# Retention plus gated MLP on one core: a hand-set engine order, two heads' scores on the row halves of TensorE, and the decay folded into q and v

## The chip, the cores and the metric

The kernel runs on one core of one Trainium2 chip. The metric is the device time of one execution in microseconds (us). Fast executions of one kernel agree within 1.5% here. The kernel before took 274.74 us in the median of four runs of one session (273.62 to 276.08). "Ratio" below means the mean time of the fast runs of one kernel over the mean of the fast runs of the kernel before, taken in the same rounds on the same chip. It is therefore not quite the ratio of the medians that are quoted beside it.

PE is TensorE (matmul on an array of 128 x 128), PEld its weight loads, PSUM is where the kernel puts the results of matmuls, DVE is VectorE, ACT is ScalarE, POOL is GpSimd, and SP is the engine that issues loads.

## The reference, cut to what matters

```python
# q, k, v: (8 batches, 8 heads, 576 positions, 64)
scores = (1/sqrt(64)) * q @ k.T
gamma  = 1 - 2.0 ** (-5 - arange(8))                  # one decay per head
ret    = scores * where(rel >= 0, gamma ** rel, 0)    # rel = query position - key position
x      = (ret @ v), heads side by side                # (8, 576, 512)

h      = gelu_tanh(x @ w_in)                          # 512 -> 1024
u, vv  = halves of h
v_n    = (vv - mean) / sqrt(var + 1e-6) * g_ln
v_s    = einsum('ts,bsd->btd', w_sg, v_n) + b_sg      # mixes the 576 positions of a batch
out    = x + (u * v_s) @ w_out
```

The decay is separable: gamma^(t-s) is gamma^t times gamma^(-s). So it can be multiplied into q, v or the result, and only the triangular mask remains for the scores.

## The kernel before: the parts that the change and the argument touch

Two batches make a pair of 9 tiles of 128 positions, and 4 pairs make 36 tiles. The fifth tile of a pair (the middle tile) straddles the two batches. Each tile passes through the following blocks, and the document uses their names throughout:

- `tp`: transposes of q and k; `sc`: scores; `ret`: masked scores, made by DVE.
- `ot`: attention output in PSUM, with one part from the carried state (`zbd`) and one from `ret` and v; `zp`: the update of the state.
- `hv` and `hu`: the two halves of the first MLP product; `vg`, `vn` (in a middle tile `vmid`): gelu and normalization of `hv`.
- `wp`: the product with w_sg, possible only once the 5 tiles of a batch are normalized; `gT`: its product with `uT`; `op`: the output.
- `wT`: the transposed w_sg, built once at the start in ten pieces, each with TensorE transposes (`wtp`) and a copy by DVE.

```python
def attn_T(i):                       # one tile: 8 transposes, then three copies out of PSUM
    ...
    nc.vector.tensor_copy(qT[:], tp[:, 0, :, :])
    nc.scalar.activation(kbd[:64, :, 0, :], tp[:64, 1, :, :], Act.Copy)   # zero-padded keys
    nc.vector.tensor_copy(kbd[64:, :, 1, :], tp[64:, 1, :, :])

def attn_S(i):                       # 8 heads in two PSUM tiles of 4, each masked by DVE
    for j in range(2):
        sc = psS.tile([128, 4, 128], F32, name="sc", tag="sc")
        for r in range(4):
            kk, hh = 2 * j + r // 2, r % 2
            nc.tensor.matmul(sc[:, r, :], s["kbd"][:, kk, hh, :], s["qT"][:, kk, :], ...)
        nc.vector.tensor_tensor(ret[:, 4*j:4*j+4, :], sc[:], msk..., op=Alu.mult)

def attn_O(i):                       # state part and two zero-padded v matmuls per head pair
    for kk in range(KK):
        nc.tensor.matmul(ot[:, kk, :n], st["zbd"][:, kk, :], s["qT"][:, kk, :n], ...)
        for hh in range(2):
            nc.tensor.matmul(ot[:, kk, :], s["vp"][:, 2*kk+hh, :], s["ret"][:, 2*kk+hh, :], ...)
    nc.vector.tensor_tensor(xT..., ot[:], ttab..., op=Alu.mult)           # decay of the queries

def build_rows():                    # rows 1/g_ln and b_sg for the w_sg product, all on DVE
    nonzero(row4[:, 0, :F2], row_t[:, :F2])                 # three passes over 4x512
    nc.vector.reciprocal(row4[:, 0, :F2], row4[:, 0, :F2])
    ...                                                     # casts and selections, 4x512, 4x576
    for t in vmid: nc.sync.dma_start(...row4b...)           # DMA them into vmid and wT

# ...
for i in range(N + 3):               # program order; the framework's scheduler reorders it
    flush(i)
    if i == SB: build_rows()
    ...loads, prep...
    attn_S(i); mlp_V(i - 1); two build_wT; attn_T(i + 1); mlp_U(i - 1); attn_O(i); attn_Z(i)
    run(2)                           # two queued units of mlp_W (two PSUM tiles) or mlp_O
```

## Time and profile before

| | before |
|---|---|
| time, median (4 runs) | 274.74 us |
| span of the profiled run | 272.1 us |
| PE busy | 227.3 us, 84% |
| DVE / ACT / POOL busy | 189.2 / 130.1 / 128.1 us |
| start of `hv` of the 8th tile | 77.4 us |
| start of `hv` of the 36th tile | 251.6 us, so 6.22 us per tile over 28 tiles |
| from there to the end | 20.5 us |

The start times of `hv` serve as a clock for the program: there is one `hv` per tile, and in steady state the distance between two of them is the time of one iteration. They cut the run into a head (up to the 8th tile), a steady part of 28 tiles, and a tail. In the kernel before the first eight start at 18.0, 23.3, 32.7, 45.3, 52.7, 60.5, 72.7 and 77.4 us.

The page of the kernel before begins with its span, the busy times, and 40 slices of the span. A digit is the busy share of a slice in tenths, and PEclk is the granted TensorE clock in tenths.

```profile
span 272.1 us, 6371 instructions
PE 227.3 (84%) x2498; PEld 171.3 (63%) x2498; DVE 189.2 (70%) x405; ACT 130.1 (48%) x230; POOL 128.1 (47%) x244
...
PE   0477747869899899987999899879998999889893
...
PEclk9999595999999999999999999999999999999998
```

After the first quarter PE is at 8 or 9 in most slices. The average of 84% hides a head in which PE is the waiting engine.

The timeline of PE in the kernel before shows one steady iteration. Columns: start in us, duration, engine, line, operation, `out<-in`, tile of the array, shape, type, count. Ends are modelled and overlap the next start, so the cost of a block is read from start to start.

```profile
101.59 0.61 PE L251 MATMUL sc<-qT,kbd_168 128*128 128x128 bf16 x8
102.04 1.03 PE L307 MATMUL hv<-w_in,xT 128*128 128x512 bf16 x4
...
104.24 0.22 PE L267 MATMUL ot<-qT,zbd_171 128*128 128x128 bf16 x1
...
104.91 0.39 PE L289 MATMUL zp<-vpad_165,qkb 128*128 128x128 bf16 x4
```

`sc` costs 102.04 - 101.59 = 0.45 us and the whole of `ot` 104.91 - 104.24 = 0.67 us. Eight full-array matmuls of 128 columns take 0.45 us, so one takes 0.056 us. These are the two blocks that the change puts on half arrays.

The table of waits of the kernel before (total us, times, longest us) has this line for the start of a `wp` block:

```profile
PE wp L349 <- DVE gT L354: 5.9, 6, 1.1
```

About 1 us is lost where such a block begins. In the head the chain of waits (start, duration, what) runs over DVE, where the row building (here `row_111` and `row4b`) and the scaling of `w_out` stand:

```profile
34.04 0.79 DVE row4b L119
34.83 0.33 DVE qT L236
35.16 3.26 DVE row_111 L114
38.42 1.49 DVE w_out L195 x4
```

The framework's scheduler had set the copy `qT`, which TensorE needs, between two parts of the row building.

### The profile page before, as it was taken

The page shows a single profiled execution, that of the slowest core. Times are in us where ns is not written, and L with a number is a line of the kernel's source. Part 1 is how long each engine was busy: PE and PEld are TensorE (multiplying, and loading weights), DVE is VectorE, ACT ScalarE, POOL GpSimd, SP SyncE. Part 2 cuts the span into 40 slices and gives each one's busy share as a digit, 9 for nine tenths or more (in the row PEclk, how much of TensorE's full clock was granted, in tenths as well). Part 3 has the DMA queues.
Part 4 walks back from the last instruction along what each step waited for, and adds up shares of the span by engine and source line. Part 5 has one row for each costly group of instructions (what it writes and reads, how often), then busy time and mean ns, then how long its engine had stood idle before and what let it go on. Part 6 is the DMA issues. An engine that isn't in the chain of part 4 may idle for free.

```text
span 272.1 us, 6371 instructions
## 1 busy us (share of the span) xinstructions
PE 227.3 (84%) x2498; PEld 171.3 (63%) x2498; DVE 189.2 (70%) x405; ACT 130.1 (48%) x230; POOL 128.1 (47%) x244
## 2 busy tenths in 40 slices
PE   0477747869899899987999899879998999889893
PEld 0245534647577687665877677657767877667561
DVE  7766797767786687656865886568777876687140
ACT  1632522344245545554465445565455476644612
POOL 7835316465267456664635575348544551131100
PEclk9999595999999999999999999999999999999998
DMA  7999999099403799398949789596966022100314
GB/s 167 273 290 232 221 198 229 4 209 193 83 4 104 200 219 213 111 279 214 193 119 211 166 168 263 167 225 126 221 173 149 2 77 80 40 4 0 116 62 173
DMA packets 120606, 42.02 MB, mean 154 GB/s; under 512 B 113824, under 2 KB 114424, under 8 KB 120576
## 3 DMA queue, kind: packets, MB, share of 16 engines
q1 hardware_dynamic: 114736, 31.51, 57.6%
q10 hardware_dynamic: 5184, 9.44, 9.5%
q0 software_dynamic: 656, 0.66, 1.4%
q8 instruction: 19, 0.31, 0.6%
q14 instruction: 11, 0.09, 0.1%
HBM read 32.80 MB, written 9.44 MB: 155 GB/s over the span
## 4 chain that ended last, share of the span: by engine, by line
PE 39%; DVE 22%; ACT 11%; DMA 8%; POOL 7%; issue 6%; SPq 3%; ACTq 2%; POOLq 0%; DVEq 0%
PE hv L307 7%; PE wp L349 6%; PE op L361 6%; PE hu L336 5%; DVE bst L312 5%; DMA vf<-in_v_dram 4%; ACT ob L367 4%; DVE xT L275 4%; ACT vg L310 4%; PE tp L234 3%; PE sc L251 3%; PE ot L271 3%; POOL rs L317 2%; ACTq L368 2%; DVE kbd_169 L239 2%
## 5 line engine op out<-in xcount | busy, mean ns | idle before, releaser
L316 POOL TENSOR_SCALAR rs<-mv 128x1 f32<-128x1 f32 x36 | 8.0, 223 | 110.0 <-DVE mv L314 105.1
L326 ACT ACTIVATE vn<-vg,nm,rs 128x512 bf16<-128x512 f32 x32 | 26.0, 814 | 50.7 <-POOL nm L319 50.7
L253 DVE TENSOR_TENSOR ret<-sc,tri 128x512 bf16<-128x512 f32 x64 | 41.0, 682 | 10.9 <-PE sc L251 10.9
L307 PE MATMUL hv<-w_in,xT 128*128 128x512 bf16 x144 | 40.3, 398 | 3.8 <-DVE xT L275 3.7
L217 POOL CAST qkb<-qk 128x1024 bf16<-128x1024 f32 x36 | 37.2, 1032 | 10.8 <-DMA qk<-in_k_dram 7.1
L312 DVE BATCH_NORM_STATS2 bst<-vg 128x6 f32<-128x512 f32 x36 | 25.0, 694 | 24.7 <-ACT vg L310 24.0
L336 PE MATMUL hu<-xT,w_in 128*128 128x128 bf16 x576 | 38.8, 221 | 1.3 <-ACT ob L367 1.3
L310 ACT ACTIVATE vg<-hv 128x512 f32<-128x512 f32 x36 | 21.5, 597 | 36.6 <-PE hv L307 30.5
L336 PEld LDWEIGHTS <-w_in 128*128 128x128 bf16 x576 | 35.1, 99 | 4.0 <-issue 2.5
L361 PE MATMUL op<-w_out,gT 128*128 128x512 bf16 x144 | 36.9, 379 | 0.0
L349 PEld LDWEIGHTS <-vn 128*128 128x128 bf16 x256 | 24.4, 97 | 18.9 <-issue 11.8
L354 DVE TENSOR_TENSOR gT<-wp,uT 128x288 bf16<-128x288 f32 x64 | 26.1, 448 | 11.3 <-PE wp L349 11.3
L234 PEld LDWEIGHTS <-qkb 128*128 128x128 bf16 x288 | 20.2, 103 | 15.5 <-POOL qkb L217 7.5
L234 PE MATMUL tp<-ident,qkb 128*128 128x128 bf16 x288 | 23.7, 229 | 6.7 <-POOL qkb L217 6.5
L275 DVE TENSOR_TENSOR xT<-ot,ttab 128x512 bf16<-128x512 f32 x36 | 24.9, 691 | 6.1 <-PE ot L271 5.4
L367 ACT ACTIVATE ob<-op 128x512 f32<-128x512 f32 x36 | 21.1, 592 | 11.2 <-PE op L364 7.2
L339 ACT ACTIVATE uT<-hu 128x512 bf16<-128x512 f32 x36 | 21.2, 590 | 10.3 <-PE hu L336 10.2
L317 POOL TENSOR_TENSOR rs<-rs,mhalf 128x1 f32<-128x1 f32 x36 | 20.6, 571 | 2.7
L307 PEld LDWEIGHTS <-xT 128*128 128x128 bf16 x144 | 12.5, 101 | 12.9 <-DVE xT L275 5.2
L236 DVE COPY qT<-tp 128x512 bf16<-128x512 bf16 x36 | 15.0, 417 | 7.2 <-PE tp L234 6.9
L361 PEld LDWEIGHTS <-gT 128*128 128x128 bf16 x144 | 12.7, 98 | 8.8 <-DVE gT L354 0.3
L364 PEld LDWEIGHTS <-xT 128*128 128x128 bf16 x144 | 11.1, 98 | 8.4
(135 smaller groups left out, 440.9 us busy)
## 6 DMA issues: line engine op xcount, KB each, us to landing
out_dram<-ob ACTq DMA_DIRECT2D x36, 256.0 KB, 2.2
qk<-in_q_dram SPq DMA_DIRECT2D x32, 256.0 KB, 4.8
qk<-in_k_dram SPq DMA_DIRECT2D x32, 256.0 KB, 4.6
vf<-in_v_dram SPq DMA_DIRECT2D x32, 256.0 KB, 4.9
wst<-in_moe_w_in_dram SPq DMA_DIRECT2D x4, 512.0 KB
wst<-in_moe_w_out_dram SPq DMA_DIRECT2D x2, 512.0 KB
qk<-in_q_dram SPq DMA_DIRECT2D x8, 128.0 KB, 5.8
qk<-in_k_dram SPq DMA_DIRECT2D x8, 128.0 KB
```

The lines of the kernel that those rows point to most:

```text
L217: nc.gpsimd.tensor_copy(qkb[:], qk[:].rearrange("p a h d -> p a (h d)"))
L234: nc.tensor.transpose(tp[:, a, kk, :], s["qkb"][:, a, kk * 128:(kk + 1) * 128], ident[:])
L253: nc.vector.tensor_tensor(ret[:, 4 * j:4 * j + 4, :], sc[:], msk[:].unsqueeze(1).to_broadcast([128, 4, 128]), op=Alu.mult)
L275: nc.vector.tensor_tensor(xTs[p][:, :, 128 * m:128 * m + 128], ot[:], ttab[:, :, t0:t0 + 128], op=Alu.mult)
L307: nc.tensor.matmul(hv[:], xTs[p][:, kk, 128 * m:128 * m + 128], w_in[:, kk, F2:], start=(kk == 0), stop=(kk == KK - 1))
L310: nc.scalar.activation(vg[:], hv[:], Act.Gelu_apprx_tanh)
L312: nc.vector.bn_stats(bst[:], vg[:])
L336: nc.tensor.matmul(hu[:, c, :], w_in[:, kk, 128 * c:128 * c + 128], xTs[p][:, kk, 128 * m:128 * m + 128], start=(kk == 0), stop=(kk == KK ...
L349: nc.tensor.matmul(ps[half][:], vns[t0 + j][e][:, 128 * c:128 * c + 128], wT[e][j][:, half * HS:(half + 1) * HS], start=(j == 0), stop=(j ...
L354: nc.vector.tensor_tensor(gTs[p][:, c, col:col + HS], ps[half][:], uTs[p][:, c, col:col + HS], op=Alu.mult)
L361: nc.tensor.matmul(op[:], gTs[p][:, c, r], w_out[:, c, :], start=(c == 0), stop=False, skip_group_check=True)
L367: nc.scalar.activation(ob[:], op[:], Act.Copy)
```

## The change

The intent is fewer instructions on DVE, the decay on GpSimd, less array time for the products that have only 64 rows or columns, and an order set by hand on every engine in place of the framework's scheduler. The diff, cut to its core:

```diff
+    ctx.enter_context(tc.manual_schedule())             # every engine runs in program order
 ...
-    sc in two tiles of 4 heads; zero-padded keys kbd; zero-padded vpads; table ttab
+    sc = psA.tile([128, 2, KK, 128], F32, ...)           # all 8 heads in one PSUM tile
+    for kk in range(KK):
+        for hh in range(2):
+            r = slice(64 * hh, 64 * hh + 64)             # each head on its row half
+            nc.tensor.matmul(sc[:, hh, kk, :], qkT[r, 1, kk, :], qkT[r, 0, kk, :], ...)
+    nc.vector.tensor_tensor(ret, sc, msk, op=mult)       # one mask of 1,024 elements
 ...
+    for kk in range(KK): matmul(ot[:, kk, :n], zbd[:, kk, :], qkT[:, 0, kk, :n], ...)
+    for kk in range(KK):
+        for hh in range(2):                              # v on column halves
+            matmul(ot[64*hh:64*hh+64, kk, :], vb[:, 2*kk+hh, :], ret[:, hh, kk, :], ...)
+    nc.scalar.activation(xT..., ot[:], Act.Copy)         # was a DVE multiplication by ttab
 ...
+    gmul(qkb[:, 0], qf, 0, m)                            # POOL: q * decay
+    gmul(vb, vf, 1, m)                                   # POOL: v * inverse decay
+    nc.vector.tensor_copy(qkT[:], tp[:])                 # one copy instead of three
 ...
+    for _ in range(12): nc.tensor.matmul(scr[:], warm[:, :128], warm[:], ...)   # warm-up
 ...
     for i in range(N + 3):
+        attn_S(i)
+        mlp_V(i - 1)                                     # hv, and gelu on ACT
+        mlp_norm(i - 2)                                  # vn on ACT; may release a wp block
+        build_wT
+        units(800)                                       # filler: wp one PSUM tile, or op
+        mlp_stats(i - 1)
+        attn_O(i); attn_T(i + 1); mlp_U(i - 1)
+        units(700)
+        attn_Z(i)
+        if i == 2: build_rows()                          # was at i == 5
+        if i == 3: scale_wout()
+        if i == SB: place_rows()                         # SB is 5: the DMAs of the rows
+        build_wT
+        units(700)
+        load(i + 4); prep(i + 2)
```

## The prediction

It was written before any kernel of the change was built or run.

> **What bounds the kernel now.** From about 77 us to the end it is TensorE. In the timeline the same blocks repeat back to back: scores 0.45 us (8 matmuls at a pitch of 56 ns), hv 0.86, transposes 0.45, hu 0.89, ot 0.67, zp 0.22. Two output tiles (1.09 each) or two wp pieces (about 1.22 each) follow, so an iteration takes 5.5 or 6.3 us. About 1 us is lost wherever a wp block begins, because its third PSUM tile waits for gT on DVE (the waits: 1.06 us). From the 8th hv (72.7 us) to the 36th (251.6) is 6.39 us per iteration; the blocks alone need about 5.7. The head is not TensorE: hv of tiles 0 to 5 start at 18, 23, 33, 45, 53 and 60 us. There it waits for DMA (230 GB/s in the windows, mostly packets under 512 B), for about 9 us of row building on DVE (one reciprocal 3.3 us), and for POOL, whose casts queue behind rs, which waits for mv (105 us in the table of waits). From 14 to 48 us the granted clock was 0.81. The tail after the last hv is 20 us.
>
> **What the change does, per tile.** DVE: two masks (1.36) become one of 1,024 elements, about 1.22 (estimate: 682 ns less 150 fixed, doubled, plus 150). Three copies from tp (0.42+0.43, and ACT 0.58) become one of about 0.7. xT (0.69) and half of zbd (0.41) leave for ACT. DVE falls from about 4.7 to 3.6 us. ACT loses 0.58, gains about 0.6 and 0.38: 3.9. POOL: two multiplications of 512 at about 1.2 (two of 256 took 1.2 together), a cast of about 0.6 and the 1.07 of rs and nm: 4.0. All stay below TensorE.
>
> TensorE: scores and the ret part of ot are half arrays. The Trainium skill ("TensorEngine Tiling (Array Packing)", Key Properties) says that tiles run in parallel, and that changing the tiling mode drains TensorE. If both halves overlapped, 0.45 us per tile would go; weight loads are as many as before, and there are about four mode changes, so I book 0.15 to 0.25 us per tile: 5 to 9 us in all. No trace here shows tiling yet.
>
> Order: wp takes one PSUM tile at a time, between other blocks, and bn is no longer ahead of what TensorE needs next. I expect the 1 us stalls to go: about 5.5 us per iteration, saving about 25 us over 28 iterations, tiling included. Head: no zero fills or ttab, fewer weights ahead of the loads, clock warm early: hv of tile 6 at about 48 us instead of about 67. The row building remains on DVE and costs several us still; DMA sets the floor (about 10 MB before tile 6 at 250 GB/s). Tail: about 17 instead of 20 us.
>
> **Sum.** 53 us for the 8th hv, 28 x 5.5 = 154, tail 18: span 225, perhaps 6 us of new stalls, plus the 3 us between span and time: **233 us**, range 217 to 253. Faster by over 2%: 0.94; within 2%: 0.04; slower: 0.02.
>
> **What would show it.** hv starts in the timeline (5.5 us apart, even); the eight score matmuls in under 0.35 us; DVE busy near 135 us, ACT near 145, POOL near 145; PE waits for gT gone; clock near 1 from the first tile.
>
> **What would make it wrong.** Mode changes costing over 0.2 us each (then tiling loses, about 245); output stores now in the same queue as the loads, holding them back; POOL being slower than scaled, so that transposes wait for qkb; ot waiting for the single long mask when the hand-set filler is too short; the row building stopping DVE in the head for its full 9 us.

## More of the kernel before

The group of the scaling in the kernel before (instances | total us, mean ns | idle before):

```profile
L195 DVE TENSOR_SCALAR w_out<-wst,g_col 128x512 bf16<-128x512 f32 x4 | 1.6, 445 | 0.0
```

## The result, and the profile after

| | before | after |
|---|---|---|
| time, median (4 runs each) | 274.74 us | 254.28 us (253.24 to 255.99) |
| ratio | | 0.925 (95%: 0.918 to 0.932), faster |
| span of the profiled run | 272.1 us | 251.5 us |
| PE / DVE busy | 227.3 / 189.2 us | 217.1 / 143.2 us |
| ACT / POOL busy | 130.1 / 128.1 us | 139.5 / 139.0 us |
| `hv` of the 8th tile starts | 77.4 us | 66.9 us |
| 28 tiles of steady part | 174.1 us, 6.22 each | 165.2 us, 5.90 each |
| tail | 20.5 us | 19.4 us |

Of the 20.6 us by which the span fell, 10.5 lie in the head, 9.0 in the steady part and 1.1 in the tail.

The direction was right. The size was 21 us off; 254.28 lies 1.3 us above the stated range of 217 to 253. The `hv` starts split the miss by the terms of the prediction's sum (which add to 234; 233 was stated):

| term | predicted | measured | difference |
|---|---|---|---|
| `hv` of the 8th tile | 53 | 66.9 | +13.9 |
| 28 tiles, with 6 us of new stalls | 154 + 6 | 165.2 | +5.2 |
| tail | 18 | 19.4 | +1.4 |
| from the profiled span to the median time | 3 | 2.8 | -0.2 |

So two thirds of the miss lie in the head, and most of the rest in the steady part. The page of the kernel after:

```profile
span 251.5 us, 6298 instructions
...
PE 217.1 (86%) x2473; PEld 152.5 (61%) x2510; DVE 143.2 (57%) x252; ACT 139.5 (55%) x254; POOL 139.0 (55%) x237
...
PE   8236809889998999989998999899989999899893
...
PEclk9756965999999999999999999999999999999999
```

The sixth digit of the PE row is 0: around 31 to 38 us TensorE stands still, although the program is well under way.

**The head.** The timeline of PE of the kernel after, around that hole:

```profile
29.86 0.81 PE L280 MATMUL hv<-w_in,xT 128*128 128x512 bf16 x3 [0.16 <-issue]
37.82 0.75 PE L186 MATMUL wtp<-ident,wnat 128*128 128x128 bf16 x5 [7.16 <-DVE wT L187]
...
40.44 1.91 PE L318 MATMUL hu<-xT,w_in 128*128 128x128 bf16 x16
...
44.03 0.81 PE L280 MATMUL hv<-w_in,xT 128*128 128x512 bf16 x3 [0.23 <-issue]
```

PE waits 7.16 us for DVE to copy a `wT` piece out of the PSUM tile that the next transposes need. The chain of waits of the kernel after (start, duration, what; "issue" is time in which nothing was waited for) says what DVE did in that time:

```profile
10.91 8.01 DMA wst<-in_moe_w_in_dram
...
19.91 0.59 ACT xT L249
...
29.80 0.69 DVE row L138
30.51 3.34 DVE row L147
...
35.34 1.23 DVE row4b L152
36.59 0.81 DVE row4b L153
37.40 0.38 DVE wT L187
...
41.29 3.59 DVE w_out L179 x4
```

In the timeline of DVE the row building runs from 28.65 to 37.40 us with no other work in between, with the reciprocal of 3.34 us in its middle, and everything behind it in program order waits, `ret` of the next tile included. The gap between `hv` of tiles 2 and 3 is 44.03 - 29.86 = 14.17 us; the tile before took 4.25. The wait explains 7.2 of the 9.9 us of excess. Much of the rest is pace: from 37 to 43 us the granted clock in the windows view was 0.50, and `hu` (16 matmuls) took 1.91 us, against 1.06 in the steady part. The Trainium skill ("TensorE: Matmul & The Clock Gate", the table "Why this matters for your kernels") advises no gaps over about 3 us between bursts of matmuls because the throughput drops after one. This trace agrees: 7.2 us of waiting, then half pace.

The first lines of the chain show a second loss: the first `hv` waits for the copy `xT` on ACT, and ACT stands in its own order behind a cast of `w_in` whose weights land at 18.9 us. The Trainium skill ("SBUF — State Buffer", "Who interferes with whom") says that DVE and GpSimd share a port pair under an exclusive lock. The groups of DVE in the kernel after, columns as before:

```profile
L228 DVE TENSOR_TENSOR ret<-sc,tri 128x1024 bf16<-128x1024 f32 x32 | 39.0, 1220 | 28.3 <-PE sc L224 28.3
...
L179 DVE TENSOR_SCALAR w_out<-wst,g_col 128x512 bf16<-128x512 f32 x4 | 3.6, 957 | 0.0
```

The same scaling of `w_out` took 445 ns each before, when POOL recorded no instruction between 37 and 41 us, and 957 ns each after, beside three POOL instructions without a gap. That fits what the page says; no run here isolated it. The kernel e10 below shows the same pattern once more: a DVE instruction on 4x1 elements took 0.15 us in the kernel after and 2.56 us in e10, where it stood beside three POOL instructions without a gap.

**The steady part.** The table of waits of the kernel after, for the lines that answer to that of before:

```profile
PE wp L330 <- ACT vn L308: 3.7, 4, 0.9
PE wp L330 <- ACT vmid L305: 3.2, 4, 0.9
```

The waits of `wp` for `gT` are gone, as predicted. In their place `wp` waits for `vn` or `vmid` from ACT, 6.9 us over the 8 blocks. ACT receives the gelu of `hv` of tile i-1 ahead of the normalization of tile i-2, which a new `wp` block needs at once.

The timeline of PE of the kernel after, one steady iteration, for comparison with that of before:

```profile
103.72 0.39 PE L241 MATMUL ot<-qkT,zbd 128*128 128x128 bf16 x4
104.03 0.41 PE L245 MATMUL ot<-ret,vb 128*64 128x128 bf16 x8
104.38 0.62 PE L212 MATMUL tp<-ident,qkb 128*128 128x128 bf16 x8
...
106.82 0.39 PE L266 MATMUL zp<-vb,qkb 128*128 128x128 bf16 x4
107.14 0.40 PE L224 MATMUL sc<-qkT 64*128 64x128 bf16 x8
107.47 1.04 PE L280 MATMUL hv<-w_in,xT 128*128 128x512 bf16 x4
...
109.89 0.30 PE L330 MATMUL wp<-wT,vmid 128*128 128x288 bf16 x1 [0.90 <-ACT vmid L305]
```

Each number is to be read from start to start:

- `sc` took 107.47 - 107.14 = 0.33 us, against 0.45. But `zp` ahead of it took 107.14 - 106.82 = 0.32 us, where four matmuls take 0.22. The difference of 0.10 is the change to the tiled mode, in which the array works as two halves. Both together cost 0.65 us; before they would cost 0.22 + 0.45 = 0.67. In tiles where another block stands ahead of `sc`, that block bears the change: a `wp` piece takes 0.71 us there, against 0.61.
- The state part of `ot` took 104.03 - 103.72 = 0.31 us for four matmuls and the v part 0.35 us for what two halves running together should do in about 0.22. Together 0.66, against 0.67 before.

The halves do run together, and what they save is given back at the changes of mode. The last line is one of the new waits.

### The profile page after: what moved, and what is told of

Its sections match the earlier page's. It is cut to its first block, busy times and chain, and to the rows that moved or that the text cites. A ratio compares the mean times of both kernels' runs of the same rounds, so it can differ in the third digit from the quotient of the medians.

```text
span 251.5 us, 6298 instructions
## 1 busy us (share of the span) xinstructions
PE 217.1 (86%) x2473; PEld 152.5 (61%) x2510; DVE 143.2 (57%) x252; ACT 139.5 (55%) x254; POOL 139.0 (55%) x237
## 4 chain that ended last, share of the span: by engine, by line
PE 71%; DVE 8%; issue 4%; POOL 4%; SPq 4%; ACT 3%; DMA 3%; ACTq 0%; POOLq 0%; DVEq 0%
PE wp L330 14%; PE hv L280 11%; PE hu L318 11%; PE op L346 11%; PE tp L212 7%; PE ot L245 5%; PE sc L224 4%; DMA wst<-in_moe_w_in_dram 3%; SPq L76 3%; PE op L343 3%; PE zp L266 3%; PE ot L241 3%; DVE w_out L179 1%; DVE row L147 1%; ACT vn L308 1%
## 5 line engine op out<-in xcount | busy, mean ns | idle before, releaser
L228 DVE TENSOR_TENSOR ret<-sc,tri 128x1024 bf16<-128x1024 f32 x32 | 39.0, 1220 | 28.3 <-PE sc L224 28.3
L330 PE MATMUL wp<-wT,vn 128*128 128x288 bf16 x256 | 42.1, 286 | 3.7 <-ACT vn L308 3.7
L280 PE MATMUL hv<-w_in,xT 128*128 128x512 bf16 x125 | 36.0, 388 | 6.5 <-ACT xT L249 4.9
L194 POOL TENSOR_TENSOR vb<-vf,gqv 128x512 bf16<-128x512 f32 x36 | 38.0, 1057 | 5.5 <-DMA vf<-in_v_dram 5.5
L194 POOL TENSOR_TENSOR qkb<-qf,gqv 128x512 bf16<-128x512 f32 x36 | 37.7, 1047 | 5.7 <-DMA qf<-in_q_dram 5.5
L283 ACT ACTIVATE vg<-hv 128x512 f32<-128x512 f32 x36 | 21.5, 597 | 31.3 <-issue 19.7
L321 ACT ACTIVATE uT<-hu 128x512 bf16<-128x512 f32 x36 | 21.5, 597 | 26.6 <-PE hu L318 26.6
L346 PE MATMUL op<-w_out,gT 128*128 128x512 bf16 x126 | 33.1, 379 | 0.9
L214 DVE COPY qkT<-tp 128x1024 bf16<-128x1024 bf16 x36 | 24.2, 671 | 11.6 <-PE tp L212 11.6
L249 ACT ACTIVATE xT<-ot 128x512 bf16<-128x512 f32 x36 | 21.3, 590 | 12.2 <-PE ot L245 11.7
L294 POOL TENSOR_TENSOR rs<-rs,mhalf 128x1 f32<-128x1 f32 x36 | 20.5, 569 | 3.0
L280 PEld LDWEIGHTS <-xT 128*128 128x128 bf16 x144 | 11.4, 99 | 17.5 <-ACT xT L249 4.8
L212 PEld LDWEIGHTS <-qkb 128*128 128x128 bf16 x288 | 16.9, 100 | 7.5 <-POOL qkb L194 3.4
```

Source lines behind the costliest of these rows:

```text
L194: nc.gpsimd.tensor_tensor(out_[:], in_[:], gqv[:, a, m, :].unsqueeze(2).to_broadcast([128, H, D]), op=Alu.mult)
L212: nc.tensor.transpose(tp[:, a, kk, :], f[:, a, kk * 128:(kk + 1) * 128], ident[:])
L214: nc.vector.tensor_copy(qkT[:], tp[:])
L228: nc.vector.tensor_tensor(ret[:].rearrange("p a k t -> p (a k) t"), sc[:].rearrange("p a k t -> p (a k) t"), msk[:].unsqueeze(1).to_broadc ...
L280: nc.tensor.matmul(hv[:], xTs[p][:, kk, 128 * m:128 * m + 128], w_in[:, kk, F2:], start=(kk == 0), stop=(kk == KK - 1))
L283: nc.scalar.activation(vg[:], hv[:], Act.Gelu_apprx_tanh)
```

## The experiments

The leading theory was that the row building in DVE's program order makes the head, that the order of ACT makes the new waits, and that tiling is worth nothing because each mode change costs about 0.11 us. The rivals were: the loads or the late first `hv` make the head; the waits cost nothing net; the tiling's cost lies in loads of half-width weights or in other parts of the blocks. All fifteen kernels gave a correct result. All times are medians of four runs; they were made in four sessions whose kernel before had medians of 274.61, 276.13, 274.41 and 276.67 us. A comparison with after that crosses sessions goes by these medians, so a difference of 1 or 2 us in it is not read. Diffs are against the kernel after unless stated, and shortened.

### e1_rows: the row building moved ahead

```diff
     load(0)
+    nc.sync.dma_start(row4[:, 0, :F2], ...); nc.sync.dma_start(row4[:, 1, :], ...)   # from load_small
 ...
+        if i == 0: build_rows()         # nonzero and reciprocal
+        if i == 1: build_rows2()        # casts and selections
-        if i == 2: build_rows()
```

> Edit: the two small row loads go right behind the first tile's loads, and the row building on DVE is cut in two and runs while DVE is idle in tiles 0 and 1, not in tile 2. Theory (the 14.2 us between the hv starts of tiles 2 and 3 is DVE held by row building, in program order): that gap falls to 7 to 9 us (then the load of tile 3, whose q landed at 32.4 us, sets it) and the time falls by 5 to 8 us, to about 247. Rival (the head is bound by DMA, the row building only fills a wait): the gap stays over 12 us and the time within 1.5 us of 254.3.

It took 250.04 us, ratio 0.908 (0.900 to 0.915), which is 4.2 us less than after. The gap between `hv` of tiles 2 and 3 fell from 14.17 to 4.83 us, so the row building did make that hole. But the gap between tiles 5 and 6 grew from 7.35 to 11.01. Timeline of PE of this kernel, columns as before:

```profile
51.80 0.40 PE L332 MATMUL wp<-wT,vmid 128*128 128x288 bf16 x1 [2.46 <-DMA wT<-row4b]
```

The first `wp` block now came so early that it ran into the DMA that places the rows. Part of the gain became a new wait.

### e2_cast: the last cast of w_in taken out of ACT's way

```diff
         if i == 0:
             nc.scalar.activation(w_in[:, 0:2, :F2], w_stage[2][2][:], Act.Copy)
-            nc.scalar.activation(w_in[:, 2:4, :F2], wst[:], Act.Copy)
 ...
             attn_T(i + 1)
+        if i == 1:
+            nc.scalar.activation(w_in[:, 2:4, :F2], wst[:], Act.Copy)
```

> Edit: the last w_in cast on ACT, which waits 6.8 us for its weights ahead of the first xT copy, moves to just before hu of tile 0. Theory: the first hv starts at about 13 us instead of 21, and the time falls by only 0 to 3 us, because tile 1's v lands at 17.5 us and the row building still stops tile 3. Rival (the late start of hv is carried through to the end): the time falls by about 8 us.

It took 253.85 us, ratio 0.922 (0.913 to 0.930): no difference from after that could be told. The first `hv` started 4.5 us sooner (16.46), but the second started at 26.32, which is 0.7 us later, and the fourth at 44.47. The late first `hv` is off the path. In the chain of this kernel v of the second tile lands at 18.0 us, and `qkb` of the third tile stands behind it and behind four fills of `vmid` on POOL until 22.5 us; the row building follows.

### e3_norm: the normalization ahead of the next gelu

```diff
-        if 1 <= i <= N: mlp_V(i - 1)
         if 2 <= i and i <= N + 1: mlp_norm(i - 2) ...
+        if 1 <= i <= N: mlp_V(i - 1)
```

> Edit: the normalization of tile i-2 is put ahead of hv and gelu of tile i-1 in program order, on ACT only. Theory (the 0.95 us waits of wp for vn and vmid, about 7 us in all over 8 blocks, come from ACT doing gelu of hv first): these waits go and the time falls by 5 to 8 us, to about 248. Rival (the wait is for nm from POOL, which is late): the waits stay, or ACT blocks gelu instead, and the time stays within 1.5 us.

It took 248.71 us, ratio 0.903 (0.897 to 0.910), 5.6 us less than after. From the 8th to the 36th `hv` it took 159.74 us in place of 165.15, that is 5.705 per tile. The waits of PE in this kernel (total us, times, longest us):

```profile
PE wp L330 <- ACT vn L308: 0.9, 1, 0.9
PE wp L330 <- ACT vmid L305: 0.7, 3, 0.2
```

5.3 of the 6.9 us of waits are gone and the steady part shrank by 5.4. So these waits lay on the path in full.

### e4_modes: more mode changes, the same matmuls

```diff
-        if m != 0:
-            for kk in range(KK): (state matmul)
-        for kk in range(KK):
+        for kk in range(KK):
+            if m != 0: (state matmul)
             for hh in range(2): (v matmul on column half)
```

> Edit: zbd and ret matmuls of ot alternate by pair of heads, so that each tile has 8 changes between full and column-halved matmuls in ot instead of 2; the matmuls are the same. Theory (each change costs about 0.10 us, which ate the gain of the halves): the ot block of a tile grows from 0.67 to about 1.2 us and the time by 15 to 22 us, to about 272. Rival (changes are free, and the halves gain nothing because weight loads set the pitch): the block stays at 0.67 us and the time within 1.5 us.

It took 276.83 us, ratio 1.006 (0.997 to 1.014): 22.5 us more than after, so the gain of the change is gone. The order adds 6 mode changes on each of 32 tiles, 192 in all, so one costs 22.5 / 192 = 0.117 us. A tile that took 5.37 us takes 6.05, which gives 0.68 / 6 = 0.113; this figure is the cleaner one, since the head of this run also shifted. Timeline of PE of this kernel:

```profile
101.34 0.22 PE L241 MATMUL ot<-qkT,zbd 128*128 128x128 bf16 x1
101.49 0.25 PE L244 MATMUL ot<-ret,vb 128*64 128x128 bf16 x2
101.67 0.23 PE L241 MATMUL ot<-qkT,zbd 128*128 128x128 bf16 x1
...
102.69 0.62 PE L212 MATMUL tp<-ident,qkb 128*128 128x128 bf16 x8
```

One full-array matmul needs 0.15 to 0.16 us up to the next start, not 0.056, and two halves 0.18. The block takes 102.69 - 101.34 = 1.35 us in place of 0.66. That the alternation alone is not the cause shows in the kernel before: there the same two kinds alternate on the full array, and 12 matmuls take 0.67 us, or 0.056 each. The Trainium skill ("TensorEngine Tiling (Array Packing)", "Key Properties") says that changing the tiling mode drains TensorE, and that tiles work in parallel. The trace agrees with both; the page gives no cost.

### e5_place: e1 and the DMAs of the rows one iteration sooner

```diff
 (e1_rows, and)
-        if i == SB: place_rows()
         build_wT
+        if i == SB - 1: place_rows()
```

> Edit: as e1_rows, and the six small copies of the rows into vmid and wT are issued one iteration earlier, behind the last wT build that they need. e1_rows took the 14.2 us gap away (4.8 us) but saved only 4 us, for the wp of the first block then waited 2.5 us for the copy of the row into wT, and the gap from hv of tile 5 to tile 6 grew from 7.4 to 11.0 us. Theory (that wait is all that gave the gain back): the gap at tile 6 falls to about 7 us and the time to 245 to 247. Rival (tile 6 is bound by the loads or by POOL): the time stays within 1.5 us of e1_rows at 250.0.

It took 246.24 us, ratio 0.893 (0.887 to 0.898), 8.0 us less than after. The gap between tiles 5 and 6 was 7.57 us, no longer 11.01, and the 8th `hv` started at 59.87 us in place of 66.91. The wait that e1 had met was 3.8 us of time.

### e6_zcol: the state part on column halves as well

```diff
             for kk in range(KK):
-                nc.tensor.matmul(ot[:, kk, :n], st["zbd"][:, kk, :], ...)
+                for hh in range(2):
+                    c = slice(64 * hh, 64 * hh + 64)
+                    nc.tensor.matmul(ot[c, kk, :n], st["zbd"][:, kk, c], ...)
```

> Edit: the zbd matmuls of ot are also done in column halves (two of 64 columns for one of 128), so that ot has no mode change inside it; 4 matmuls and 4 weight loads more per tile. Theory (a change costs 0.117 us, from e4_modes: 22.5 us over 192 changes; halves run in pairs at full pitch): ot falls from 0.67 to about 0.57 us, and the time by 3 to 4.5 us, to about 250.5. Rival (halves cost by the number of weight loads): ot grows by 0.1 to 0.2 us and the time rises by 3 us or more.

It took 254.53 us, ratio 0.922: nothing. The expectation of a gain was a miscount of mine. The change of mode only moves from the middle of `ot` to its start, and one change in and one out remain. The trace shows the move: the last four matmuls of a `wp` piece ahead of `ot` take 0.58 us, against 0.49 in after, and the state part takes 0.25, against 0.32. The run still says something. Four more loads and four more half matmuls per tile cost no measurable time, so the rival that blames half-width loads falls. The Trainium skill ("TensorEngine Tiling (Array Packing)", "Restrictions") says that column tiling disables the fast weight load. In the trace of after, a load of 64 columns (`vb`) took 112 ns on average, against 101 ns for a full one (`zbd`). That fits the page: half the width made the load no cheaper.

### e7_padv: v back to zero-padded full-array matmuls

```diff
+    vpads: three tiles [128, H, 128], zero outside the head's own 64 columns, filled by POOL
-    nc.tensor.matmul(ot[64*hh:64*hh+64, kk, :], s["vb"][:, 2*kk+hh, :], s["ret"][:, hh, kk, :], ...)
+    nc.tensor.matmul(ot[:, kk, :],              s["vp"][:, 2*kk+hh, :], s["ret"][:, hh, kk, :], ...)
```

> Edit: the ret part of ot goes back to whole-array matmuls with zero-padded v, as in the kernel before; scores keep their row halves. Theory (column halves win 0.225 us per tile and lose two changes of 0.117 us): the time stays within 1.5 us of 254.3. Rival 1 (the halves are the gain of the change): it rises by about 8 us. Rival 2 (they cost more than they win): it falls by over 3 us.

It took 254.37 us, ratio 0.922: nothing, and the 5.37 us tile still takes 5.37. The timeline of PE:

```profile
93.36 0.39 PE L249 MATMUL ot<-qkT,zbd 128*128 128x128 bf16 x4
93.58 0.61 PE L253 MATMUL ot<-ret,vpad 128*128 128x128 bf16 x8
94.03 0.61 PE L220 MATMUL tp<-ident,qkb 128*128 128x128 bf16 x8
```

Without the mode changes `ot` takes 0.22 + 0.45 = 0.67 us; with column halves it took 0.66. If eight halved matmuls run in pairs at full pitch, they save 0.225 us; two changes that eat this up cost 0.112 each, which agrees with the 0.113 of e4. For the column halves the break-even lies here. No run put the scores back on the full array; for the row halves it is read from the trace alone (0.65 us against 0.67).

### e8_nowarm: no warm-up matmuls

```diff
-    for _ in range(12):
-        nc.tensor.matmul(scr[:], warm[:, :128], warm[:], start=True, stop=True, ...)
```

> Edit: the 12 warm-up matmuls are taken out. Theory (the clock granted from 14 to 48 us was 0.71, so the warm-up is lost again while TensorE waits in the head, and the head is bound by DMA and DVE anyway): within 1 us of 254.3. Rival (they keep the clock up where it counts): slower by 2 us or more.

It took 254.53 us, ratio 0.922: nothing. In the kernel after, the transposes right behind the warm-up are quick (8 in 0.63 us modelled, against 1.03 without it). But PE then waits 3.2 us for POOL and 4.9 us for ACT, and the first `hv` runs at half pace in both kernels: 1.49 us for 3 recorded matmuls after, 1.89 us for 4 here, against 1.03 for 4 in the steady part. So the early full pace was gone before it mattered. The same table of the Trainium skill ("TensorE: Matmul & The Clock Gate", "Why this matters for your kernels") that asks for 4 us of continuous work also asks for no gaps over about 3 us, and this head has gaps of 3.2 and 4.9 us.

### e9_sched: one mode change fewer per tile

```diff
-        attn_S(i) at the head of the iteration; attn_T(i + 1) behind attn_O(i)
+        attn_T(i + 1) ahead of the first filler; attn_S(i + 1) right behind attn_O(i)
```

> Edit: transposes of tile i+1 go ahead of the filler, and the scores of tile i+1 come right behind ot of tile i, so that row halves follow column halves directly: 3 mode changes per tile instead of 4, the same matmuls. (e6_zcol did not test this: counted again, its ot still has one change in and one out, so the 3 to 4.5 us that I expected of it were a miscount, and 0 is what 0.112 us per change gives.) Theory (each change costs 0.112 us, whichever modes it joins): the time falls by about 4 us, to about 250.3, and hv starts lie 5.26 us apart where they lay 5.37. Rival (a direct change between halves costs as much as two through the whole array, or only the entry into a mode costs): no change within 1 us; or the new order makes TensorE wait for qkT, and it is slower.

It took 257.09 us, ratio 0.936 (0.930 to 0.941), 2.8 us more than after. The steady part gained (162.3 us for 28 tiles, against 165.2), but the 8th `hv` started 5.6 us later, at 72.50. In the head the transposes now stand ahead of other work and wait for `qkb` from POOL, 8.7 us in all, where after had 3.2. The gain of the steady part is not the one that was expected: a tile that took 5.37 us takes 5.40, and the waits of `wp` for `vn` and `vmid` fell from 6.9 to 4.5 us. The run mixes several effects; e14 tests the order without the loss in the head and without most of these waits.

### e10_rpn: rows, placing and normalization together

```diff
 (e5_place and e3_norm)
```

> Edit: e5_place and e3_norm together. Theory (the two losses lie in different stretches, head and steady state): the gains add, 8.0 and 5.6 us, to about 240.7. Rival (the first block's waits share the time): 243 or more.

It took 241.26 us, ratio 0.879 (0.874 to 0.884). The gains add: 8.0 + 5.6 = 13.6 us less than after would be 240.7. The 8th `hv` starts at 59.66 us and 28 tiles take 159.74 us. The long stall is gone, and the granted clock from 37 to 43 us is 1.00 in place of 0.50; from 12 to 24 us it is still 0.50. But the row building has not left the path wholly. The chain of waits of this kernel:

```profile
6.20 11.40 DMA kf<-in_k_dram
...
21.85 2.56 DVE sel L152
...
36.29 2.01 DVE w_out L181 x4
```

The second half of the row building runs from 21.5 to 26.7 us on DVE, with the slow `sel` instruction named above in it. The copy `qkT` of the third tile stands behind it, and PE waits 0.8 us for that copy. The page:

```profile
span 238.9 us, 6301 instructions
...
PE   7316898999999999999999999999999999999893
```

From the eighth slice on, up to the tail, PE is at 9 throughout; in after there were eights in it at regular distances.

### e11_head: e10, the cast of e2, and w_out loaded and scaled later

```diff
 (e10_rpn and e2_cast, and)
-        if i == 3: scale_wout()
+        if i == 6: scale_wout()
+        load_wout() behind the loads of iteration 1
```

> Edit: e10_rpn, the last w_in cast as in e2_cast, and w_out loaded after tile 5 instead of tile 3 and scaled at tile 6. Theory (with the row building gone, the head is bound by bytes: 1 MB less ahead of tiles 4 and 5 is worth up to 4 us, and the early first hv now counts): 1 to 4 us below e10_rpn. Rival (latency of the chain through POOL bounds the head): within 1 us of e10_rpn.

It took 243.51 us, ratio 0.886 (0.881 to 0.892), 2.3 us more than e10. Tiles 3 to 5 started 1 to 2 us sooner, but the gap between tiles 6 and 7 grew from 5.84 to 9.50. The timeline (DVE and PE) of this kernel:

```profile
51.05 3.35 DVE L181 TENSOR_SCALAR w_out<-wst,g_col 128x512 bf16<-128x512 f32 x4
...
55.19 0.65 PE L332 MATMUL wp<-wT,vn 128*128 128x288 bf16 x4 [1.34 <-DVE gT L336]
```

The scaling met the first `wp` block and held `gT`, and `wp` waited for its PSUM tiles.

### e12_all: e11 with the order of e9

```diff
 (e11_head and e9_sched)
```

> Edit: e11_head and e9_sched together. Expected: about 4 us below e11_head if e9_sched holds, near 235.

It took 248.17 us, ratio 0.903 (0.898 to 0.908). The 8th `hv` starts at 67.65 us, 8.0 later than in e10; the steady part takes 159.6 us. As in e9 the transposes wait for `qkb`. The new order spoils the head also where the long stall is gone; e12 has the late scaling of e11 in it as well.

### e13_cast: e10 and the cast of e2

```diff
 (e10_rpn and e2_cast)
```

> Edit: e10_rpn with the last w_in cast moved as in e2_cast, w_out as before. Theory (with the row building out of the way the late first hv is the next delay, but the loads of tiles 1 and 2 follow close behind it): 0 to 2 us below e10_rpn at 241.3. Rival 1 (the 4 to 5 us of an earlier first hv are carried to the end): 4 us or more below. Rival 2 (the cast, not the w_out scaling, made e11_head slow): 2 us or more above.

It took 242.12 us, ratio 0.876 (0.871 to 0.882), not to be told from e10. The 8th `hv` started at 62.16 us in the profiled run, the slowest of the four. No gain of the cast shows here either.

### e14_sched9: e10, with the order of e9 from tile 9 on

```diff
 (e10_rpn, and)
-        attn_S(i) for every i
+        attn_S(i) at the head of the iteration while i < 9
+        from tile 9 on: attn_T(i + 1) ahead of the filler, attn_S(i + 1) right behind attn_O(i)
```

> Edit: e10_rpn with the order of e9_sched from tile 9 on only. Theory (a mode change less per tile is worth 0.1 us where no new wait is made): hv of tiles 10 to 35 come about 2.5 us sooner in all, and the time is 1.5 to 3 us below e10_rpn, at 238.3 to 239.8. Rival (the gain of e9_sched's steady state was chance, or its waits for qkT eat it): within 1 us of e10_rpn.

It took 240.65 us, ratio 0.872 (0.866 to 0.877). By the medians that is 0.6 us below e10, by the ratios (0.872 against 0.879, intervals that overlap) about 2 us; it is not separable from e10. The trace is clearer. From the 8th to the 36th `hv` it took 159.71 us, against 159.74. Timeline of PE of this kernel:

```profile
95.18 0.41 PE L247 MATMUL ot<-ret,vb 128*64 128x128 bf16 x8
95.53 0.40 PE L226 MATMUL sc<-qkT 64*128 64x128 bf16 x8
```

One change now leads straight from column halves to row halves, and single tiles do gain 0.10 us (5.61 against 5.71, 5.27 against 5.37). Others lose as much. At a middle tile, `zp` needs only 64 rows and also runs in the row mode. In the old order it lay just ahead of `sc`, shared its mode and ran between its matmuls; now it stands alone and pays two changes of its own, and that tile takes 5.70 us, against 5.60. There are also three new waits of `sc` for `qkT`, 1.3 us in all, where e10 had 1.1 us of waits of `ot` for `vb`. The sum is zero.

### e15_both: e14 and the cast of e2

```diff
 (e14_sched9 and e2_cast)
```

> Edit: e13_cast and e14_sched9 together. Expected: their gains add; between 237 and 240 us.

It took 241.45 us, ratio 0.874 (0.870 to 0.879), not better than e14 and not separable from e10.

**The best version shown** is e10, with e14 beside it: 241.26 us is 0.949 of the median of after (254.28), and 0.879 of before by the ratio. e10 is the one to keep, because it changes only the places of a few calls and no gain of e14 over it is shown.

## Why the prediction was right or wrong, point by point

- **"From about 77 us to the end it is TensorE": right.** The 28 steady tiles at 5.705 us in e3 and e10 are the sum of the blocks that the prediction put at "about 5.7". The gain of the change in the steady part, 9.0 us, is the loss of stalls, not shorter blocks: tiles with the same blocks and no wait took 5.72 and 5.61 us before, and 5.71 and 5.60 after. The listed waits of PE in these 28 tiles fell from 11.5 to 6.6 us. The other 4 us are, as read from the starts, mostly pauses inside the `wp` blocks of before that are too short for the list.
- **"I expect the 1 us stalls to go": right about those, and the allowance for others was right in size, by luck.** "Perhaps 6 us of new stalls" became 6.9 us of waits of `wp` for `vn` and `vmid`, which the prediction doesn't name. e3 removed 5.3 us of them and gained 5.6.
- **"saving about 25 us over 28 iterations": wrong, 9.0.** The base of 6.39 us per iteration took the 7th `hv` for the 8th; it was 6.22, which is 4.8 us less to save. The new stalls that the sum books apart took 5.4, and the tiling that gave nothing 5.7.
- **"I book 0.15 to 0.25 us per tile: 5 to 9 us in all": wrong, it is zero.** This is one failed term of the sum. The step that failed is the size of a mode change. With about 0.11 us each (e4, e7) and "about four mode changes" per tile, the changes cost about 0.45 us, which is what the halves save: 0.225 in `sc` and 0.225 in `ot`. The prediction counted the changes correctly and named the threshold "over 0.2 us each" for tiling to lose; by its own figures, 0.45 / 4 = 0.11 us is where it stops gaining. Its 28 x 5.5 becomes 28 x 5.7. That is 5.6 us more, and the steady part was 5.2 us off.
- **"hv of tile 6 at about 48" and "53 us for the 8th hv": wrong, 61.1 and 66.9.** This is the failed term that cost most, 13.9 us. The prediction said "The row building remains on DVE and costs several us still", and listed "the row building stopping DVE in the head for its full 9 us" among what would make it wrong. That is what happened: 8.75 us in one piece, with 7.2 us of waiting on PE and then half pace. What was missed in the reading of the diff is that the row building moved from iteration 5 to iteration 2, and that a hand-set order lets nothing pass it; `ret` of the next tile and the `wT` copies stand behind it. In the kernel before the reciprocal took as long (3.33 us) and was on the chain too, but the scheduler had set other DVE work, such as the copy `qT`, between its parts. e5 shows 7.0 us of earlier start of the 8th `hv`, and 8.0 of time. The miscount enters here too: the prediction put `hv` of tile 6 in the kernel before at "about 67", where it started at 72.7. How much of the 53 us rests on that can't be told, since the prediction also gives DMA as the floor; the start did fall by 10.5 us, from 77.4, and not by the 19.7 that 72.7 to 53 would be.
- **The other 6.7 us of the head are not settled.** In e10 the 8th `hv` starts at 59.7 us, not 53. On its chain stand k of the second tile, which lands at 17.6 us, the second half of the row building (to 26.7 us, a wait of 0.8 us on PE) and the scaling of `w_out` (2.0 us). PE waits 2.8 and 3.1 us for `qkb`, and tiles in the ramp take 4.25 us or more, with two `wT` pieces of about 0.4 us each in them. That the remaining 6.7 us consist of these is argued from the trace and was not tested. They don't simply add: in e15 the slow `sel` instruction took 0.15 us, and its 8th `hv` still started at 60.3. Three attempts to shorten the head further (e11, e12, e13) failed.
- **Tail: 19.4 against 18, near enough.**
- **Per-instruction costs: right.** The long mask took 1.220 us (predicted 1.22; its 150 ns of fixed cost fit the kernel before, where 288 columns took 448 ns and 512 took 682), the single copy 0.671 (0.7). DVE was busy 143 us (135), ACT 139.5 (145), POOL 139 (145). The eight scores took 0.33 us ("under 0.35"), but that sign did not show a gain, since the cost lies outside the block.
- **"Clock near 1 from the first tile": wrong.** The granted clock from 14 to 48 us was 0.71, lower than the 0.81 of before. The long stall is the cause as far as is shown: without it e5 has 0.82. The warm-up is worth nothing (e8).
- **Stores in the same queue as loads: did not matter.** No wait for loads of that kind stands among the longest in the steady part.
- **Not shown:** what the hand-set order alone is worth. No run separates it from the other parts of the change.

## What to carry to other kernels

Before putting a block on half arrays, count the mode changes it brings: here one costs as much as two full-array matmuls of 128 columns, so eight halved matmuls that need one change in and one out gain next to nothing. When the order of every engine is set by hand, each long once-only job (a reciprocal row, a scaling, a cast) must be placed by what stands behind it on its own engine, and one job moved may run into the next. A stage start such as a `wp` block waits for the last small step of its input, so that step belongs ahead of work for the next tile.

## What the Trainium skill lacked or had wrong

- "TensorEngine Tiling (Array Packing)" states that a mode change drains TensorE but gives no cost. Here it was 0.113 us (e4, single tiles) to 0.117 us (e4, whole time) for changes between full array and column halves; row halves showed 0.10 to 0.11.
- The same page has no advice to put blocks of one mode side by side. A 64-row state update ran between the score matmuls at a middle tile, and that tile took 5.60 us, against 5.70 when an order parted them (e14).
- "TensorE: Matmul & The Clock Gate" warns that the clock events of a trace are unreliable on trn2, but not that slow stretches can be recorded at full clock. In e8 the record shows 1.00 from 20 to 24 us, while the first `hv` took 1.89 us for 4 matmuls, against 1.03 in the steady part.
- No page gives a time for the reciprocal on VectorE. One of 4x512 float elements took 3.34 us, against 0.40 us for a pass with one input (`row_t`, L136) and 0.68 us for one with two (L137) over the same shape.
